# Reordering the hand-over from S to the first block in batch 0 of a fused attention and channel-mix kernel

**Chip and metric.** One core of one Trainium2 chip. PE is the matrix engine (TensorE) and PEld its weight load, DVE VectorE, ACT ScalarE, POOL GpSimd, SP SyncE. All times are device microseconds (us), the time of a run being that of the core from launch to end. The span in a profile, from the first to the last instruction, is about 1.85 us shorter than the time of the same run.

## The reference

Cross-covariance attention on three inputs of 4 x 6208 x 256, followed by a channel mix with a shift by one row:

```
s = (k / |k|)^T (q / |q|)            # 256 x 256 per batch, norms over the rows
a = softmax(s);  x = v @ a           # 6208 x 256 per batch
xk = mu_k*x + (1-mu_k)*x_prev        # x_prev: x, one row later; xr likewise with mu_r
out = sigmoid(xr @ w_r) * (relu(xk @ w_k)**2 @ w_v)     # w_k 256 x 1024, w_v 1024 x 256
```

Nothing of x can be had before S of that batch is complete. For batches 1 to 3 the kernel computes S beside the blocks of the batch before. For batch 0 there is nothing to work on beside it, so the time between the last row of S and the first full stream of matmuls is spent waiting. The change is about that time.

## The kernel before

S of batch 0 is summed in 14 row groups: 0 is the 64 rows left over, 11 (`DIRECT`) the last full one, 12 and 13 (`LAST`) are of half size. What the change touches:

```python
# the last group: q and k diagonals, norms, then the off-diagonal part of S
if last:
    for s in range(n):
        for ih in range(2):          # L192: q and k diagonal
            ...
    diagonal()                       # DVE: sum of q squares from the diagonal
    norms_last()                     # PE: k squares of the last group
for s in range(n):
    for ih in range(2):              # L199: off-diagonal
        ...
def norms_first():                   # called before the cast of the last group
    bank[0] = ps.tile([P, 8], F32, name="bank", tag="xT_ps", bufs=2)
    for h in range(2): nc.tensor.matmul(bank[0][:, h:h + 1], rowsum["acc"][...], ones_f, ...)
    for g in [0] + list(range(DIRECT, LAST)):
        norms_of(g)
... # (cut)
root(1); root(0)                                   # ACT: square roots of the norms
nc.scalar.activation(gate, ones[:, 0:1], AF.Exp)   # ACT: loads exp's table
nc.tensor.transpose(bank[0][:, 4:8], mu_rows, ident_f[:4, :4])
keep_warm(2)                                       # PE: junk matmuls
turn_half, take_half = v_first()
invert_first(0)                                    # DVE
evac_first()                                       # DVE: S, times 1/|q|, out of PSUM
turn_half(0)                                       # PE: first half of v's block 0 turned
turn()                                             # PE: S turned
turn_half(1)
go = v_transpose_pe(1, nc.scalar.copy)             # PE: v's block 1 turned; go() is its copy, on ACT
keep_warm(3)
invert_first(1)
take_half(0, nc.vector.tensor_copy)
nc.vector.tensor_copy(mu_t, bank[0][:, 4:8])
nc.vector.tensor_scalar_add(less, mu_t, -1.0)
difference(0)                                      # DVE: v minus the row before, first half
exp()                                              # ACT
take_half(1, nc.scalar.copy)
go()
weigh_first(0); weigh_first(1)                     # DVE: softmax weights a_sb
difference(1)
for a in range(2):                                 # two halves of the first block's 512 rows
    for ih in range(2): product(a, ih)             # PE: x_ps; ACT: xT from it
    for dh in range(2): mix_first("xk", a, dh)     # DVE: xk
```

After this come the first matmuls with w_k ("up"). The results (`res`) of the first blocks are held back (`HOLD = 4`) and stored from about 95 us on, so that their stores stay out of the way of the loads.

## Time and profile before

| | before |
|---|---|
| time | 505.73 (median of 3 runs, 505.73 to 505.91) |
| profiled run | 505.47, span 503.7 |
| PE busy | 479.2 of 503.7 us (95%) |
| first matmul of group 11 | 32.59 |
| up matmul after the last wait of the hand-over | 49.52 |

Two lines of the profile's page of the kernel before, busy time by engine and the shares of the chain that ended last:

```profile
PE 479.2 (95%) x3372; PEld 331.1 (66%) x3432; DVE 428.9 (85%) x790; ACT 428.7 (85%) x870; POOL 97.0 (19%) x143
PE 90%; DMA 4%; ACT 2%; DVE 2%; issue 1%; SPq 0%; ACTq 0%; DVEq 0%
```

PE is the bound, and what can be gained lies where PE isn't. (3372 matmul records against 3432 weight loads: some matmuls are missing from this trace, so its PE share reads a little low.) Two moments serve as marks below. "Start" is the first matmul of group 11, which comes when the loads and casts let it. "**Hand-over**" is the time from there to the first matmul of block 1's up product after its xk (`49.52 PE kT_ps` in the chain of waits of before): 49.52 - 32.59 = 16.93. From there on PE hardly waits.

### The profile page before, as it was taken

To read this page: it belongs to the slowest core of one execution; us is meant where nothing else is said; L and a number is where in the kernel's file an instruction comes from. 1 tells how busy PE (TensorE), PEld (TensorE's weight loads), DVE (VectorE), ACT (ScalarE), POOL (GpSimd) and SP (SyncE) were. 2 spreads that over 40 slices of the span, in tenths; PEclk is the share of its full clock that TensorE was granted. 3 is DMA by queue.
4 is the path that set the end of the run, shared out by engine and by line. 5 is a ranking of instruction groups with operands and counts; after the bars stand their busy time and mean duration, and the time that the engine had idled before them with its cause. 6 is when DMAs were issued, how large, how long until landed. Compare 5 with 4: busy or idle time off the path is not lost.

```text
span 503.7 us, 9236 instructions
## 1 busy us (share of the span) xinstructions
PE 479.2 (95%) x3372; PEld 331.1 (66%) x3432; DVE 428.9 (85%) x790; ACT 428.7 (85%) x870; POOL 97.0 (19%) x143
## 2 busy tenths in 40 slices
PE   2689999999999999999999999999999999999996
PEld 1345677677666666776676676666666666666675
DVE  2778899999988998899889899899888787878784
ACT  4778999899989989888999898988888878788784
POOL 0044332222233122122123322110031010000000
PEclk9999999999999999999999999999999999999999
DMA  8999999999799999997799999983295857345123
GB/s 332 417 309 189 197 191 176 193 203 213 149 180 176 209 164 175 148 205 117 140 196 140 197 173 185 162 144 75 64 201 102 161 88 152 78 103 88 55 72 105
DMA packets 131558, 83.46 MB, mean 166 GB/s; under 512 B 50548, under 2 KB 125624, under 8 KB 130488
## 3 DMA queue, kind: packets, MB, share of 16 engines
q0 software_dynamic: 55840, 33.01, 49.4%
q1 hardware_dynamic: 75352, 49.59, 40.4%
q8 instruction: 27, 0.44, 0.4%
q10 hardware_dynamic: 320, 0.26, 0.2%
q14 instruction: 19, 0.16, 0.1%
HBM read 78.71 MB, written 25.43 MB: 207 GB/s over the span
## 4 chain that ended last, share of the span: by engine, by line
PE 90%; DMA 4%; ACT 2%; DVE 2%; issue 1%; SPq 0%; ACTq 0%; DVEq 0%
PE vr_ps L598 33%; PE kT_ps L566 30%; PE vr_ps L594 10%; PE xT_ps L460 8%; PE s_ps L288 6%; DMA f<-in_k_dram 4%; ACT k L160 1%; ACT qk L155 1%; PE s_ps L199 1%; PE st_ps L348 0%; PE y_ps L638 0%; DVE xk L551 0%; DVE k L167 0%; DVE kk L579 0%; ACT kr L508 0%
## 5 line engine op out<-in xcount | busy, mean ns | idle before, releaser
L571 ACT ACTIVATE kr<-kT_ps 128x512 bf16<-128x512 f32 (+1 forms) x390 | 234.7, 604 | 33.6 <-PE kT_ps L566 29.8
L598 PE MATMUL vr_ps<-w_v_sb,kk 128*128 128x256 bf16 x1536 | 230.3, 273 | 0.1
L566 PE MATMUL kT_ps<-xk,w_k_sb 128*128 128x512 bf16 (+1 forms) x721 | 217.3, 377 | 0.4 <-DVE xk L551 0.2
L598 PEld LDWEIGHTS <-kk 128*128 128x128 bf16 x1536 | 150.3, 98 | 57.3
L579 DVE TENSOR_TENSOR kk<-kr 128x2048 bf16<-128x2048 bf16 (+1 forms) x148 | 125.7, 850 | 0.2 <-ACT kr L571 0.2
L608 DVE SCALAR_TENSOR_TENSOR res<-res,vr_ps 128x256 f32<-128x256 f32 x192 | 79.9, 416 | 50.6 <-ACT res L607 50.6
L566 PEld LDWEIGHTS <-w_k_sb 128*128 128x128 bf16 x780 | 75.5, 98 | 27.5 <-issue 0.6
L607 ACT ACTIVATE res<-vr_ps 128x256 f32<-128x256 f32 x192 | 76.6, 399 | 1.3 <-PE vr_ps L598 1.3
L594 PE MATMUL vr_ps<-w_r_sb,xr 128*128 128x256 bf16 x384 | 73.3, 273 | 2.8
L462 ACT CAST xT<-xT_ps 128x512 bf16<-128x512 f32 x94 | 55.8, 594 | 20.0 <-PE xT_ps L460 19.7
L551 DVE SCALAR_TENSOR_TENSOR xr<-delta,mu_t,xT 128x512 bf16<-128x512 bf16 x94 | 70.0, 745 | 0.0
L551 DVE SCALAR_TENSOR_TENSOR xk<-delta,mu_t,xT 128x512 bf16<-128x512 bf16 x94 | 69.9, 745 | 0.0
L594 PEld LDWEIGHTS <-xr 128*128 128x128 bf16 x384 | 37.6, 98 | 44.5 <-issue 0.2
L133 POOL DMA_DIRECT2D qk<-in_q_dram x39 | 26.0, 667 | 169.5 <-ACT kr L571 152.1
L460 PE MATMUL xT_ps<-vT,a_sb 128*128 128x512 bf16 x188 | 55.9, 379 | 0.0
L288 PE MATMUL s_ps<-qk 128*128 128x256 bf16 (+1 forms) x294 | 55.8, 273 | 0.0
L249 ACT ACTIVATE sq<-qk 128x1024 bf16<-128x1024 bf16 x48 | 51.0, 1062 | 0.0
L403 POOL DMA_DIRECT2D v_bf<-in_v_dram x47 | 35.7, 761 | 66.4 <-DMA vT<-v_bf 49.5
L199 PE MATMUL s_ps<-qk 128*128 128x384 bf16 (+2 forms) x98 | 19.7, 347 | 16.1 <-ACT qk L155 15.3
L541 DVE TENSOR_TENSOR delta<-xT 128x1024 bf16<-128x1024 bf16 x47 | 32.2, 686 | 1.1 <-ACT xT L462 1.1
L288 PEld LDWEIGHTS <-qk 128*128 128x128 bf16 (+1 forms) x294 | 28.5, 98 | 5.6 <-issue 0.8
L133 POOL DMA_DIRECT2D qk<-in_k_dram x39 | 25.9, 664 | 4.0 <-DMA w_k_sb<-in_moe_w_k_dram 2.7
(114 smaller groups left out, 252.3 us busy)
## 6 DMA issues: line engine op xcount, KB each, us to landing
out_dram<-res SPq DMA_DIRECT2D x47, 512.0 KB, 4.8
v_bf<-in_v_dram POOLq DMA_DIRECT2D x47, 256.0 KB, 7.6
qk<-in_q_dram POOLq DMA_DIRECT2D x36, 256.0 KB, 5.8
qk<-in_k_dram POOLq DMA_DIRECT2D x36, 256.0 KB, 7.4
f<-in_q_dram SPq DMA_DIRECT2D x4, 1024.0 KB, 13.1
f<-in_k_dram SPq DMA_DIRECT2D x4, 1024.0 KB, 11.0
f<-in_q_dram SPq DMA_DIRECT2D x3, 512.0 KB, 7.7
f<-in_k_dram SPq DMA_DIRECT2D x3, 512.0 KB, 6.1
```

The source lines that it names most:

```text
L133: nc.gpsimd.dma_start(rows_at(qk, b, g, i)[:rows, :n], qk_src(t, b, g))
L288: nc.tensor.matmul(s_ps[:, ih, :], rows_at(qk, b, g, 0)[:rows, s, ih * P:(ih + 1) * P], rows_at(qk, b, g, 1)[:rows, s, :], start=t0 and ih ...
L460: nc.tensor.matmul(xT_ps, a_sb[:, b, ih, dh * P:(dh + 1) * P], vT[:, :, ih, :], start=ih == 0, stop=ih == 1)
L462: nc.scalar.copy(xT[:, dh, 1:], xT_ps)
L551: nc.vector.scalar_tensor_tensor(o[:, dh], st[i, "d"][:, dh], mu[:, dh:dh + 1], st[i, "x"][:, dh, :M], op0=OP.mult, op1=OP.add)
L566: nc.tensor.matmul(kT_ps[:, :m], w_k_sb[:, dh, fh * P:(fh + 1) * P], xk[:, dh, :m], start=dh == 0, stop=dh == 1)
L571: nc.scalar.activation(kr, kT_ps[:, :m], AF.Relu, scale=0.5 ** 0.5)
L579: nc.vector.tensor_tensor(st[i, "kk"][:, fh // 4 * 4 + lo:fh + 1, :m], kr, kr, op=OP.mult)
L594: nc.tensor.matmul(vr_ps[:, D:], xr[:, dh, s * P:(s + 1) * P], w_r_sb[:, dh, :], start=dh == 0, stop=dh == 1)
L598: nc.tensor.matmul(vr_ps[:, :D], kk[:, fh, s * P:(s + 1) * P], w_v_sb[:, fh, :], start=fh == 0, stop=fh == 7)
L607: nc.scalar.activation(res[:, s], vr_ps[:, D:], AF.Tanh, scale=0.5)
L608: nc.vector.scalar_tensor_tensor(res[:, s], res[:, s], 1.0, vr_ps[:, :D], op0=OP.add, op1=OP.mult)
```

## The change

Five moves: (1) the norm matmuls of all groups up to 11 before S of group 12 rather than after it; (2) in the last group the norms of groups 12 and 13 and the turn of mu behind the q diagonal, with mu copied by ACT from a bank of its own, and the off-diagonals ordered by half; (3) both halves of v turned ahead of S, the second copied by ACT before exp rather than after; (4) x by output half, and the second xT copied as two halves; (5) three junk matmuls fewer.

```diff
+        for s, ih in [(s, ih) for ih in range(2) for s in range(n)] if last else \
+                [(s, ih) for s in range(n) for ih in range(2)]:      # off-diagonals by half
...
-        for g in [0] + list(range(DIRECT, LAST)):
+        for g in (0, DIRECT):
             norms_of(g)
...
-        norms_of(LAST)
+        mu_ps = ps.tile([P, 4], F32, name="mu_ps", tag="kT_ps", bufs=3)
+        nc.tensor.transpose(mu_ps, mu_rows, ident_f[:4, :4])
+        for g in range(DIRECT + 1, LAST + 1):
+            norms_of(g)
+        nc.scalar.copy(mu_t, mu_ps)
+        nc.vector.tensor_scalar_add(less, mu_t, -1.0)
...
-            for t, src in zip(pairs[a], (...)):
-                for dh in range(2):
+            for dh in range(2):
+                for t, src in zip(pairs[a], (...)):
                     nc.tensor.matmul(t[:, dh], a_sb[...], src, ...)
             if ih:
-                for dh in (0, 1) if a == 0 else (slice(0, 2),):
+                for dh in (0, 1):
                     nc.scalar.copy(xT[...], pairs[a][0][:, dh])
...
-        if g == LAST:
-            norms_first()
         group_cast(g, pending)
+        if g == DIRECT + 1:
+            norms_first()
...
-    nc.tensor.transpose(bank[0][:, 4:8], mu_rows, ident_f[:4, :4])
-    keep_warm(2)
...
     turn_half(0)
+    turn_half(1)
+    take_half(1, nc.scalar.copy)
     turn()
-    turn_half(1)
+    keep_warm(2)
     go = v_transpose_pe(1, nc.scalar.copy)
-    keep_warm(3)
     invert_first(1)
     take_half(0, nc.vector.tensor_copy)
-    nc.vector.tensor_copy(mu_t, bank[0][:, 4:8])
-    nc.vector.tensor_scalar_add(less, mu_t, -1.0)
     difference(0)
     exp()
-    take_half(1, nc.scalar.copy)
     go()
```

More of the change, by code (lines that the diff above doesn't have):

```diff
@@ L195, in cov_first @@
             norms_last()
-        for s in range(n):
-            for ih in range(2):
-                c = slice(P, 3 * P) if last else slice(ih * P, ih * P + 3 * P)
-                nc.tensor.matmul(cov[0][ih][:, c], row[:rows, s, at[ih]:at[ih] + P], row[:rows, s, c],
-                                 start=g == 1 and s == 0, stop=last and s == n - 1, skip_group_check=True)
+        for s, ih in [(s, ih) for ih in range(2) for s in range(n)] if last else \
+                [(s, ih) for s in range(n) for ih in range(2)]:
+            c = slice(P, 3 * P) if last else slice(ih * P, ih * P + 3 * P)
+            nc.tensor.matmul(cov[0][ih][:, c], row[:rows, s, at[ih]:at[ih] + P], row[:rows, s, c],
+                             start=g == 1 and s == 0, stop=last and s == n - 1, skip_group_check=True)
     def norms_first():
-        bank[0] = ps.tile([P, 8], F32, name="bank", tag="xT_ps", bufs=2)
+        bank[0] = ps.tile([P, 4], F32, name="bank", tag="xT_ps", bufs=2)
         for h in range(2):
@@ L479, in product @@
                               for tag, bufs in ((("vr_ps", 2), ("vr_ps", 2)), (("s_ps", 1), ("xT_ps", 2)))[a]])
-            for t, src in zip(pairs[a], (vT0[:, ih, a * H + 1:(a + 1) * H + 1], dv[:, ih, a * H:(a + 1) * H])):
-                for dh in range(2):
+            for dh in range(2):
+                for t, src in zip(pairs[a], (vT0[:, ih, a * H + 1:(a + 1) * H + 1], dv[:, ih, a * H:(a + 1) * H])):
                     nc.tensor.matmul(t[:, dh], a_sb[:, 0, ih, dh * P:(dh + 1) * P], src,
```

## The prediction

> **What bounds the kernel now.** I read the page first, then the chain of waits in order of time from 0 to 75 us, then the timelines of single engines from 32 to 50 us. From about 49.5 us to the end the chain is PE, one matmul after another, with pieces of "issue" of 0.05 us. Before 32 us it is loads and casts. The diff touches only what lies between: the hand-over of batch 0 from S to the first block. What it saves there moves the whole PE-bound rest forward, if nothing between 42 and 49.5 us holds it back.
>
> The end of S, in PE's timeline:
>
> ```profile
> 33.40 1.45 PE L199 MATMUL s_ps<-qk 128*128 128x384 bf16 x7
> 34.69 0.50 PE L206 MATMUL bank<-ones_f,k_acc 128*128 128x1 f32 x4
> 35.13 0.20 PE L217 MATMUL bank<-ones,k_left 64*128 64x1 bf16 x2
> 35.26 0.45 PE L217 MATMUL bank<-ones,k 128*128 128x1 bf16 x12
> 35.57 0.38 PE L192 MATMUL s_ps<-qk 128*128 128x128 bf16 x4
> 35.79 0.24 PE L217 MATMUL bank<-ones,k 128*128 128x1 bf16 x4
> ```
>
> The norm matmuls (L206, L217) stand between the last full groups of S and the q diagonal (L192), although the last cast (DVE L157, 34.26 for 0.41 us) has been done since 34.67. The diagonal feeds the rest.
>
> The same stretch on ACT:
>
> ```profile
> 36.07 0.17 ACT L317 ACTIVATE rn<-bank 128x2 f32<-128x2 f32 x1 [1.14 <-PE bank L217]
> 36.49 0.20 ACT L317 ACTIVATE rn<-rn 128x2 f32<-128x2 f32 x1 [0.24 <-DVE dg L313]
> 36.71 1.28 ACT L734 ACT_TABLE_LOAD   x1
> 38.00 0.21 ACT L734 ACTIVATE gate<-ones 128x1 bf16<-128x1 bf16 x1
> 38.61 0.47 ACT L356 ACTIVATE e_sb<-st_ps,rn 128x256 f32<-128x256 f32 x1 [0.40 <-PE st_ps L348]
> ...
> 39.95 0.59 ACT L442 COPY vT<-vT_ps 128x512 bf16<-128x512 bf16 x1 [0.32 <-DVE sm L368]
> 40.43 1.02 ACT L428 COPY vT<-vT_ps 128x1024 bf16<-128x1024 bf16 x1
> 41.33 1.40 ACT L486 CAST xT<-x_ps 128x256 bf16<-128x256 f32 x3
> ```
>
> ACT is the path from 39.95 to 41.33: it copies the second half of v and block 1's v before the first x. And on DVE:
>
> ```profile
> 38.83 0.42 DVE L442 COPY vT<-vT_ps 128x512 bf16<-128x512 bf16 x1 [0.48 <-PE vT_ps L439]
> 39.17 0.15 DVE L747 COPY mu_t<-bank 128x4 f32<-128x4 f32 x1
> 39.36 0.17 DVE L748 TENSOR_SCALAR less<-mu_t 128x4 f32<-128x4 f32 x1
> 39.44 0.42 DVE L474 TENSOR_TENSOR delta<-vT 128x512 bf16<-128x512 bf16 x1
> 39.77 0.16 DVE L368 RECIPROCAL sm<-sm 128x1 f32<-128x1 f32 x1
> 39.97 0.35 DVE L369 TENSOR_SCALAR a_sb<-e_sb,sm 128x256 bf16<-128x256 f32 x1
> 40.23 0.15 DVE L368 RECIPROCAL sm<-sm 128x1 f32<-128x1 f32 x1
> 40.42 0.35 DVE L369 TENSOR_SCALAR a_sb<-e_sb,sm 128x256 bf16<-128x256 f32 x1
> ```
>
> exp had delivered its first sum by 39.17, but DVE reaches its reciprocal at 39.77: copy, mu, less and delta stand in the queue before it.
>
> **The Trainium skill.** "PSUM — Partial Sum Buffer", section "PSUM bank collisions raise a hardware error", has two engines kept apart by bank and quadrant, "not by address". The trace agrees in effect: the off-diagonal matmul at 36.29 waits for DVE's read of other columns of the bank, and the copy at 38.83 of half 0 waits for PE's turns of half 1. I use this three times. "TensorE: Matmul & The Clock Gate", section "The HAM clock gate", has a whole idle window of some 3.4 us bring the clock down; here it stays at 1.00 in every 2 us from 36 to 52 with PE idle 0.5 us at most, and the change removes three of five junk matmuls, so this bears on a rival. "ScalarE: Activation LUTs", section "What ACT_TABLE_LOAD costs", measures about 1283 ns; the trace has 1.28.
>
> **Part by part.** All in us; the new times are estimates from the durations and start-to-start distances of the trace.
>
> *Norms sooner.* Eight matmuls of group 11 run from 32.59 at 0.162; group 12's four start only at 34.05, on a cast ending 33.99. So PE idles about 0.16, which the early norms fill. They take 34.69 to 35.46, so 0.77, of which the hole swallows 0.16; the four of group 12 (4 x 0.025 = 0.10) go behind the diagonal. New: 33.89 + 0.77 = 34.67, then 4 x 0.162, so the diagonal starts at 35.32 instead of 35.57: **0.26 sooner**, not the 0.88 that the norms occupy, since most only trade places with other PE work.
>
> *Behind the diagonal* come the mu turn (about 0.16 to the next matmul, as at 36.92) and eight norm columns (0.25): the first root starts near 36.1, as before. The second needs the diagonal at 36.49 - 0.26 = 36.23; the mu copy and the root ahead of it cost some 0.03. Both mu rows have landed at 34.3 by the trace's record, so nothing waits. The second root is at **36.26, 0.23 sooner**. Off-diagonals by half save about 0.1 on PE, but they end before the evacuation, which waits for the root: nothing.
>
> *Both halves of v ahead of S.* The second half of v, issued at 32.68, lands near 36.8, so its turns run at 36.87 to 37.1, before S needs PE (37.74 - 0.23). ACT: table, gate (37.77), then take_half(1) at 37.99; its distance to the next was 0.48, so exp starts at 38.47 rather than 38.61. ACT's table load is now the bound there. exp ends near 39.5, and the 1.02 copy of block 1's v starts there, not at 40.43: ACT is free at 40.4, 0.9 sooner.
>
> *DVE then is the path.* take_half(0) reads the same bank and tile as take_half(1), so it starts at 37.99 + 0.59 + 0.03 = 38.61. Before: 38.83. mu and less, worth 0.18 (delta could have begun at 39.26, not 39.44), are gone from here. delta 39.07, sm 39.41 (+0.34), a_sb 39.60 (+0.19), second a_sb 40.06 (+0.46). Against 39.97 and 40.42 that is **0.36 sooner**. The first x of the second input half runs at 40.47 (0.41 after a_sb).
>
> *x by output half.* ACT waits for a whole bank. x's second half used to be the second matmul of that group and becomes the third (+0.11). So xT starts at 40.47 + 0.23 + 0.27 + 0.04 = 41.01 (before 41.33), xk at 41.44 (before 41.76): the order costs 0.11. For a = 1, the last x matmul ends near 41.85 (before 42.10), and xT split in two lets the third xk start after 0.40 instead of 0.59. The third and fourth xk are 0.44 sooner: 42.32 and 42.72 for 42.76 and 43.16. The fourth one releases the matmul at 43.69, after which kr, xT, delta (46.32), kk and xk (48.06) follow without slack to PE at 49.52. So **0.44** reaches the PE-bound part.
>
> Sum: 0.23 (diagonal and root) + 0.13 (DVE queue; the rest of what it gains is given back waiting for ACT's copy) - 0.04 (wait for the third matmul, net of PE being free sooner) + 0.12 (split xT) = 0.44. 505.73 - 0.45 = **505.28 us**, 0.09%.
>
> **Rivals.**
> 1. *w_k takes over.* It is issued at 34.10 and lands late:
>
> ```profile
> w_k_sb<-in_moe_w_k_dram POOLq DMA_DIRECT2D x1, 512.0 KB, 7.8
> ```
>
> That is 41.95, and the first up matmul runs at 42.30. If the two copies don't wait for each other or xT needs one matmul only, xk would come 0.6 to 0.9 sooner and w_k would cap the gain near 0.6: 505.1. Against it: the waits by bank seen above. In my main case w_k lands about as the first xk ends, 41.93, and the second matmul still waits for its xk.
> 2. *The mu turn holds the roots.* Mu and eight norms now stand before the first root, which stands before the second on ACT's queue. If fp32 turn and wait cost 0.3 more than I took, all the diagonal's gain is lost: 505.5. For it: fp32 matmuls here are slow to be followed (0.18 after L206).
> 3. *PE cools down* without three junk matmuls: a microsecond or more at half clock, 506.5 or above. Against it: PE still works in every microsecond; no gap should exceed 1.0.
> 4. *Hidden anyway*: a load due between 44 and 50 us ends the wait instead. Against it: block 2's v lands at 46.4 and is turned at 47.66, w_v at 49.0 and is first used at 50.8; both have over 0.7 of slack.
>
> **Range and chances.** Rivals 1 and 2 set the edges of the range: 504.90 to 505.60; runs of before spread 0.18. Rival 3 or something unseen is most of what lies outside. 2% is 10 us, far beyond anything in 10 us of hand-over: faster 0.005, same 0.985, slower 0.01.
>
> **What would show it.** Right: the diagonal (L192) starts near 35.3; the second root near 36.25; no gap but the table load between the root and exp on ACT; DVE's copy L442 starts just after ACT's copy L442 ends; the first xk at about 41.4, PE's clock 1.00 throughout, and the first matmul after the last wait at about 49.1. Wrong: the first root after 36.3 (rival 2); the first up matmul waiting for w_k's load with xk long done (rival 1); a clock under 1.00 at 36 to 44 us (rival 3); or 0.4 sooner at 43.5 us and nothing at 50 (rival 4).

## The result

| | before | changed |
|---|---|---|
| time, same rounds | 505.82 (4 runs, 505.73 to 505.98) | 505.62 (4 runs, 505.10 to 506.12) |
| ratio | 1 | 0.9996, 95% interval 0.9978 to 1.0013 |
| profiled run: time, span | 505.47, 503.7 | 505.44, 503.7 |

A ratio here and below is the mean time of one kernel's fast runs over that of the other's of the same rounds, so not quite the ratio of the medians quoted. The median lies just above the range of the prediction (504.90 to 505.60), and a gain of 0.2 us isn't clear of the noise. Striking beside it: the changed kernel's four runs spread over 1.0 us, those of before over 0.25.

The page of the changed kernel, the same two lines:

```profile
PE 481.4 (96%) x3429; PEld 330.8 (66%) x3429; DVE 429.0 (85%) x789; ACT 428.8 (85%) x872; POOL 97.3 (19%) x143
PE 87%; DMA 6%; ACT 3%; DVE 2%; issue 1%; SPq 1%; ACTq 0%; DVEq 0%
```

PE is no busier in truth (3429 records are seen here of what was 3372 there). The new thing is in the chain: DMA's share has grown from 4% to 6%. A DMA has entered the chain of waits where the prediction saw matmuls alone. In the chain itself (start, us, what) it is a turn of v (`vT`), issued at 113.25 and landed at 129.97:

```profile
113.25 16.72 DMA vT<-v_bf
```

First the hand-over. PE's timeline of the changed kernel (start, duration, engine, line, operation; all line numbers of this kernel are some 5 higher than in before from L200 on):

```profile
34.92 0.81 PE L199 MATMUL s_ps<-qk 128*128 128x384 bf16 x4
35.57 0.39 PE L192 MATMUL s_ps<-qk 128*128 128x128 bf16 x4
35.89 0.22 PE L223 MATMUL mu_ps<-ident_f,mu_rows 4*128 4x4 f32 x1
36.04 0.35 PE L217 MATMUL bank<-ones,k 128*128 128x1 bf16 x8
```

The diagonal follows S of group 12 (34.92) at once, and mu and the rest of the norms come behind it. It starts at 35.57, to the hundredth where it was before. But this run's loads came later: its group 11 began at 32.84, not 32.59. Measured from there the diagonal is at 2.73 instead of 2.98. This is why all marks below are counted from that start.

ACT of the changed kernel:

```profile
38.00 0.21 ACT L739 ACTIVATE gate<-ones 128x1 bf16<-128x1 bf16 x1
38.11 0.57 ACT L447 COPY vT<-vT_ps 128x512 bf16<-128x512 bf16 x1
38.61 0.47 ACT L361 ACTIVATE e_sb<-st_ps,rn 128x256 f32<-128x256 f32 x1
...
39.58 1.01 ACT L433 COPY vT<-vT_ps 128x1024 bf16<-128x1024 bf16 x1
41.13 0.65 ACT L491 CAST xT<-x_ps 128x256 bf16<-128x256 f32 x2 [0.54 <-PE x_ps L487]
```

The second half of v is copied before exp and not after, and it starts only 0.11 after the gate starts, although the gate takes 0.21: neighbours on ACT overlap. ACT then waits 0.54 for PE before the first xT; it is no longer the path. DVE is:

```profile
38.72 0.43 DVE L447 COPY vT<-vT_ps 128x512 bf16<-128x512 bf16 x1 [0.20 <-ACT vT L447]
...
39.71 0.37 DVE L374 TENSOR_SCALAR a_sb<-e_sb,sm 128x256 bf16<-128x256 f32 x1
40.18 0.35 DVE L374 TENSOR_SCALAR a_sb<-e_sb,sm 128x256 bf16<-128x256 f32 x1
41.54 1.75 DVE L498 SCALAR_TENSOR_TENSOR xk<-x_ps,less,xT 128x256 bf16<-128x256 f32 x4 [0.67 <-ACT xT L491]
```

All marks counted from the first matmul of group 11, with the prediction's times minus 32.59 (its frame) for comparison:

| mark | before | predicted | changed |
|---|---|---|---|
| q diagonal, PE L192 | 2.98 | 2.73 | 2.73 |
| first root, ACT | 3.48 | about 3.5 | 3.58 |
| second root, ACT | 3.89 | 3.67 | 3.65 |
| ACT's copy of v's second half | 7.35 | 5.40 | 5.27 |
| exp, ACT | 6.02 | 5.88 | 5.77 |
| DVE's copy of v's first half | 6.24 | 6.02 | 5.87 |
| second a_sb, DVE | 7.83 | 7.47 | 7.33 |
| first xT, ACT | 8.74 | 8.42 | 8.28 |
| fourth xk, DVE | 10.57 | 10.13 | 9.97 |
| hand-over | 16.93 | 16.49 | 16.33 |

The last mark in the chains of before and of the changed kernel (start, us, what):

```profile
49.52 0.38 PE kT_ps L566
```

```profile
49.17 0.38 PE kT_ps L571
```

The hand-over went as foretold and then some: 0.60 shorter, not 0.44. And yet the last result of the full blocks started on DVE at 497.92 against 497.93 in before (below, "last result"). 0.25 of the 0.60 was gone before it began (the later start). The rest was lost later. ACT's timeline of the changed kernel at 114 us:

```profile
114.28 0.38 ACT L612 ACTIVATE res<-vr_ps 128x256 f32<-128x256 f32 x1 [1.03 <-DMA out_dram<-res]
```

ACT waited 1.03 us for the store of an earlier, held result to leave the buffer that it wanted. In before no engine waits for a store between 100 and 145 us. The store is only part of it: counted from result 20, results 24 to 27 come 1.13 later than in before, but from result 28 on only 0.20 is left of that. The turned v of the chain above adds the rest. I mark this stretch by DVE's result number 20, counted from 0 (near 104 us), and number 36 (near 144): it takes 40.33 in before and 40.68 in the changed kernel. From result 36 to the last it is 353.67 in both. (In all eighteen profiles below it is 353.67 or 353.68, and 54.40 from the end of the hand-over to result 20.)

So the last result of every profile can be put together from three terms and a constant: last result = start + hand-over + late loss + 448.41, where **late loss** is what the stretch takes beyond 40.33, and 448.41 comes from before (497.93 - 32.59 - 16.93). For the changed kernel: 32.84 + 16.33 + 0.35 + 448.41 = 497.93, measured 497.92. The experiments check this sum and ask what each term depends on.

### The profile page after: what moved, and what is told of

The parts are those of the page before. It is cut to its first block, busy times and chain, and to the rows that moved or that the text cites. A ratio compares the mean times of both kernels' runs of the same rounds, so it can differ in the third digit from the quotient of the medians.

```text
span 503.7 us, 9289 instructions
## 1 busy us (share of the span) xinstructions
PE 481.4 (96%) x3429; PEld 330.8 (66%) x3429; DVE 429.0 (85%) x789; ACT 428.8 (85%) x872; POOL 97.3 (19%) x143
## 4 chain that ended last, share of the span: by engine, by line
PE 87%; DMA 6%; ACT 3%; DVE 2%; issue 1%; SPq 1%; ACTq 0%; DVEq 0%
PE vr_ps L603 32%; PE kT_ps L571 32%; PE vr_ps L599 8%; PE xT_ps L465 8%; PE s_ps L293 6%; DMA vT<-v_bf 3%; DMA f<-in_k_dram 3%; ACT k L160 1%; ACT qk L155 1%; SPq L125 1%; PE s_ps L199 0%; PE y_ps L643 0%; DVE xk L556 0%; PE st_ps L353 0%; DVE k L167 0%
## 5 line engine op out<-in xcount | busy, mean ns | idle before, releaser
L571 PE MATMUL kT_ps<-xk,w_k_sb 128*128 128x512 bf16 (+1 forms) x780 | 230.0, 377 | 0.2 <-DVE xk L556 0.2
```

Source lines behind the costliest of these rows:

```text
L571: nc.tensor.matmul(kT_ps[:, :m], w_k_sb[:, dh, fh * P:(fh + 1) * P], xk[:, dh, :m], start=dh == 0, stop=dh == 1)
```

## The experiments

Two theories on the missing gain: **A**, that transfers fall behind by chance in either kernel, and **B**, that the earlier hand-over brings this about. The first account of all profiles (us; "time" is that of the profiled run itself):

| kernel | start | hand-over | late loss | sum + 448.41 | last result | time |
|---|---|---|---|---|---|---|
| before | 32.59 | 16.93 | 0 | 497.93 | 497.93 | 505.47 |
| null | 32.63 | 16.92 | 0 | 497.96 | 497.95 | 505.59 |
| null2 | 32.81 | 16.96 | 0 | 498.18 | 498.18 | 505.72 |
| null3 | 32.98 | 17.00 | 0 | 498.39 | 498.38 | 506.03 |
| null4 | 32.93 | 17.17 | 0 | 498.51 | 498.50 | 506.06 |
| null5 | 32.84 | 16.93 | 0 | 498.18 | 498.17 | 505.75 |
| null6 | 32.94 | 16.93 | 0 | 498.28 | 498.27 | 505.84 |
| cut_before | 33.04 | 16.92 | 0 | 498.37 | 498.36 | 505.97 |
| changed, first | 32.84 | 16.33 | 0.35 | 497.93 | 497.92 | 505.44 |
| again | 32.73 | 16.81 | 1.72 | 499.67 | 499.65 | 507.25 |
| again2 | 32.97 | 16.37 | 0 | 497.75 | 497.74 | 505.28 |
| cut_after | 32.72 | 16.54 | 0.49 | 498.16 | 498.15 | 505.67 |
| more | 32.81 | 16.32 | 0 | 497.54 | 497.53 | 505.04 |
| joint | 32.83 | 16.85 | 0 | 498.09 | 498.09 | 505.64 |
| x_order | 32.74 | 17.18 | 0 | 498.33 | 498.32 | 505.86 |
| norms_only | 32.49 | 16.68 | 0.72 | 498.30 | 498.28 | 505.82 |
| turn_only | 32.73 | 16.81 | 0.80 | 498.75 | 498.75 | 506.36 |
| best | 32.75 | 16.21 | 0 | 497.37 | 497.36 | 504.90 |

The sum holds within 0.02 for all eighteen, so up to the last result the three terms are all there is. From there to the time of the run it is another 7.51 to 7.65.

### null and again: both kernels unchanged, once more

No edit; both kernels again, in the same rounds, to see how far each repeats.

> The kernel before again, for the spread. Theory A (what the changed kernel lost between 104 and 141 us is chance: a backlog of transfers that comes and goes from run to run): the time spreads by up to 1 us here too, 505.2 to 506.3, and some profile of it shows waits for a store or for a turned v between 90 and 145 us. Theory B (the change itself brings the backlog on): spread stays near 0.25 us around 505.8, and its profile has no such wait. From the first matmul of group 11 to the last wait before the PE-bound part (the up matmul at 49.52) it takes 16.93 us again.

> The changed kernel again. Both theories: from the first matmul of group 11 to the up matmul after the last wait 16.33 us, 0.60 less than before (49.17 - 32.84 against 49.52 - 32.59). Theory A: the backlog is not the same as in its first profile, and the median is some 0.3 to 0.6 us under that of the kernel before once the runs are more than four. Theory B: the same waits between 104 and 141 us again, and a median within 0.2 us of before.

Measured: null 506.07 (five runs, 505.59 to 506.93), ratio 1.0011 (0.9998 to 1.0024); again 505.52 (six runs, 504.95 to 507.25), ratio 1.0003 (0.9989 to 1.0017); before beside them 505.69 (11 runs). So the kernel before doesn't repeat within 0.18 us, as its first three runs made me think. By the letter, null's spread fits theory A; again's median, 0.17 under before, and its wait for a store fit theory B. The changed kernel reaches 504.95, which before never does, and 507.25, which before doesn't either. The profile fell on that 507.25. PE's timeline of again at the first up matmuls, and ACT's at 116 us:

```profile
42.73 0.61 PE L511 MATMUL kT_ps<-xk,w_k_sb 128*128 128x256 bf16 x4 [0.78 <-DMA w_k_sb<-in_moe_w_k_dram]
```

```profile
116.15 0.39 ACT L612 ACTIVATE res<-vr_ps 128x256 f32<-128x256 f32 x1 [2.54 <-DMA out_dram<-res]
```

Two waits, each for a DMA. The first is rival 1 of the prediction: w_k landed at 42.68, the first xk was there, and the hand-over took 16.81 instead of 16.33. The second cost 1.72: results 24 to 27 come 2.64 later, and 0.93 of that is caught up by result 28.

The kernel before has the first wait too, with next to no harm. PE's timeline of null:

```profile
42.64 0.61 PE L506 MATMUL kT_ps<-xk,w_k_sb 128*128 128x256 bf16 x4 [0.29 <-DMA w_k_sb<-in_moe_w_k_dram]
```

Here w_k landed at 42.59, and the hand-over is 16.92 all the same, because the fourth xk comes at 10.57 and the path runs through it. In eight profiles of before, w_k lands 9.1 to 10.1 after the start; the latest (null2) costs its hand-over 0.03. In the changed kernel a landing at 9.41 (more) costs nothing, one at 9.44 (again2) 0.04, with block 1's v holding the fourth xk back by the same 0.04, and one at 9.95 (again) 0.48. The change took the slack that hid it.

### norms_only and turn_only: one part of the change alone

```diff
 # norms_only: before, and only
-        for g in [0] + list(range(DIRECT, LAST)):
+        for g in (0, DIRECT):
-        norms_of(LAST)
+        for g in range(DIRECT + 1, LAST + 1):
+            norms_of(g)
-        if g == LAST: norms_first()
         group_cast(g, pending)
+        if g == DIRECT + 1: norms_first()
 # turn_only: before, and only
-    keep_warm(2)
     turn_half(0)
-    turn()
     turn_half(1)
+    take_half(1, nc.scalar.copy)
+    turn()
+    keep_warm(2)
     go = v_transpose_pe(1, nc.scalar.copy)
-    keep_warm(3)
...
-    take_half(1, nc.scalar.copy)
```

> Only the early norms, mu and v as before. My prediction's step: the diagonal's first matmul 0.26 sooner after group 11's first matmul (2.72 us instead of 2.98), the second root 0.26 sooner, and, since ACT then waits for exp's operand anyway and every later step hangs on it, 0.2 to 0.26 sooner at the up matmul after the last wait (16.67 to 16.73 us). Rival (ACT and DVE queues after exp hide it, as they are in the same order): under 0.1.

> Only the order of v's turns and copies and the junk matmuls; norms, mu and x as before. My theory: the diagonal is not moved (2.98), ACT's copy of v's second half now ends before exp, so exp starts some 0.1 us later after the second root than before (2.12 us from root to exp before), the first a_sb waits for it, and the up matmul after the last wait comes 0.1 to 0.3 us sooner since ACT's long copy is gone from the path. Rival (the long ACT copy was the whole path): 0.45 or more.

Measured: norms_only 505.62 (ratio 1.0001), turn_only 505.65 (1.0002), both within noise of before. By the hand-over each gains: norms_only 16.68, so 0.25 sooner, just what the diagonal gained; turn_only 16.81, so 0.12. Together 0.37 of 0.60. The remaining 0.23 is left to mu off DVE's queue, the split xT and x by output half; x_order and joint below show the last two alone (-0.11 and 0.20), no run shows mu alone. One expectation of turn_only failed: from the second root to exp it takes 2.12 as before, not 0.1 more. And each lost its gain again on the way, in the same place. ACT's timelines of norms_only and of turn_only:

```profile
114.79 0.38 ACT L608 ACTIVATE res<-vr_ps 128x256 f32<-128x256 f32 x1 [1.54 <-DMA out_dram<-res]
```

```profile
115.25 0.38 ACT L607 ACTIVATE res<-vr_ps 128x256 f32<-128x256 f32 x1 [1.63 <-DMA out_dram<-res]
```

Late losses of 0.72 and 0.80.

### cut_before and cut_after: the first eight stores cut to one row

Their outputs are wrong, which doesn't matter for the times. What waits for a held result's store should then wait no more.

```diff
-                    nc.sync.dma_start(*stores.pop(0))
+                    to, frm = stores.pop(0)
+                    few[0] += 1
+                    nc.sync.dma_start(*((to[0:1, 0:1], frm[0:1, 0:1]) if few[0] <= 8 else (to, frm)))
```

> The kernel before with its first eight stores (issued from 94 us on) cut to one row, so their 4 MB do not move; the result is wrong on purpose. Theory A (chance decides in each run whether the transfers fall behind from about 55 us on; where they do, block 6 waits for a held result's store and the gain of the hand-over is used up): everything to 94 us as before, 16.93 us to the up matmul after the last wait; no wait for a store whether or not the transfers are behind; 505.4 to 505.6 with little spread, since the profiles of before had no such wait anyway. Theory B (the stores are not the cause, other transfers are): spread of over 1 us remains.

> The changed kernel with the same cut; the result is wrong on purpose. Theory A: the hand-over's gain, 0.5 to 0.6 us where w_k lands in time and about 0.1 where it lands late, stays to the end: median 504.9 to 505.4, some 0.3 to 0.5 under the cut kernel before, and no run over 505.8. Theory B: runs over 506 remain and the two cut kernels have the same median within 0.1.

Measured: cut_before 506.07 (ratio 1.0009, 0.9993 to 1.0024), no sooner than before, which missed what I expected of it; cut_after 505.58 (0.9997, 0.9983 to 1.0010), above the 504.9 to 505.4 that theory A had expected. The 0.49 between them is near the gain in hand-over, but no more than a hint, as the intervals overlap. The profiles say more. cut_before had no late loss; its profiled run (505.97) is long by its start, at 33.04 the latest of all. In cut_after the waits for stores are gone and the late loss is still 0.49: in its table of waits PE now waits 0.3 us for turned v (`vT`), another transfer. Its chain goes through that turn of v (92.67 to 109.88). So stores are not the only thing that comes late; turned v does too.

cut_after's hand-over of 16.54 has a cause of its own: its chain of waits (start, us, what) comes from block 1's v. Beside it the same place in null4, of which more below:

```profile
33.53 6.09 DMA v_bf<-in_v_dram
```

```profile
33.73 6.10 DMA v_bf<-in_v_dram
```

Both landed 6.90 after the start, 39.62 and 39.83, and both cost about the same: 0.21 to cut_after's hand-over (16.54 for 16.33) and 0.24 to null4's (17.17 for 16.93). This sensitivity, unlike that to w_k, is old.

### x_order: x in the order of before

```diff
-            for dh in range(2):
-                for t, src in zip(pairs[a], (...)):
+            for t, src in zip(pairs[a], (...)):
+                for dh in range(2):
```

> The changed kernel with only the order of the x matmuls of before (both halves of x, then both of its difference). My prediction had the new order cost 0.11 because a copy waits for the whole bank: so the first xT copy and the first xk come 0.11 sooner after group 11's first matmul than the changed kernel's 8.28 and 8.69, that is at 8.17 and 8.58. Rival (the copy waits for its own half): they come no sooner or later by up to 0.11. At the fourth xk (9.97) little is left of either, as DVE has become the bound there: 9.86 to 9.97.

From the second a_sb to the first xT takes 0.84, against 0.95 in the changed kernel: the order "by output half" costs 0.11, as the prediction had it. The 0.11 is still there at the fourth xk (2.53 against 2.64 from the second a_sb), where the expectation had thought it hidden. The gain isn't seen in the time, since two loads came late. ACT's and PE's timelines of x_order:

```profile
38.53 0.59 ACT L447 COPY vT<-vT_ps 128x512 bf16<-128x512 bf16 x1 [0.43 <-PE vT_ps L444]
```

```profile
43.11 0.61 PE L511 MATMUL kT_ps<-xk,w_k_sb 128*128 128x256 bf16 x4 [0.60 <-DMA w_k_sb<-in_moe_w_k_dram]
```

The second half of v landed at 38.05, where it lands between 36.8 and 37.7 in all other profiles. Its turn now stands ahead of S on PE, so exp was 0.51 later than in the changed kernel (6.28 for 5.77). w_k at 43.06 came on top. The hand-over of 17.18 is the longest of all, by 0.01 over null4, and its chain leads to w_k, which set it. What turning both halves ahead of S risks is the other part: the fourth xk at 10.40 instead of 9.97.

### best: a version meant to beat both

The changed kernel with x in the order of before, w_k in two tiles and two loads of half the size (the first up matmuls need the first half only), and two more tiles for held results.

```diff
-    w_k_sb = const.tile([P, 2, DF], BF16, name="w_k_sb")
+    w_k_sb = [const.tile([P, 2, DF // 2], BF16, name=f"w_k{n}_sb") for n in range(2)]
...
-    nc.gpsimd.dma_start(w_k_sb, moe_w_k.rearrange("(ko ki) f -> ki ko f", ki=P))
+    for n in range(2):
+        nc.gpsimd.dma_start(w_k_sb[n], moe_w_k.rearrange(...)[:, :, n * DF // 2:(n + 1) * DF // 2])
...
+            extra = name == "res" and extras[0] > 0     # the first two res tiles
+            t = pn.tile(shape, dtype, name="res_x", tag="res_x", bufs=2) if extra else \
...
-    HOLD = 4                                            # and max(0, i - 3)
+    HOLD = 6                                            # and max(0, i - 5)
```

> A version meant to beat both: the changed kernel with the x order of before, w_k loaded in two tiles (the half that the first up matmuls need first), and two more result tiles with two more blocks held, so that a store has some 30 us to land instead of 10. Theory A: w_k's first half lands near 40 us and is never waited for, the up matmul after the last wait comes at 16.2 to 16.35 us in every run, no block waits for a store: median 504.8 to 505.1, spread under 0.5. Theory B: the hand-over is as said, but the median stays at 505.4 or more with runs over 506.

Measured: 504.90 (five runs, 504.59 to 505.63) against 505.68, ratio 0.9986 (0.9974 to 0.9999), correct. It is the only kernel here whose interval lies below 1, by a hair. The first half of w_k landed at 41.01 (before: 41.95 for the whole), no up matmul waits for it, the hand-over is 16.21 and the late loss 0. The expected spread of under 0.5 was missed (1.04). From the second a_sb to the first xT it takes 0.84 and to the fourth xk 2.53, as in x_order, so the 0.11 or 0.12 by which its hand-over beats 16.32 and 16.33 is accounted for by the order of x: that part of the change was a loss. What its other parts are worth, one profile can't tell.

### null2 and again2: both unchanged, with five rounds

> The kernel before a further time, to see whether its transfers too fall behind. Theory A (chance for both kernels; the hand-over of before has slack for its loads, that of the changed kernel has none): 16.93 us from group 11's first matmul to the up matmul after the last wait whatever the landing of v and w_k, up to about 42.6 for w_k; the stretch from result 20 to result 36 takes 40.33 us where the transfers keep up and 0.3 to 1.7 more where they do not. Theory B (only the changed kernel's transfers fall behind): 40.33 again.

> The changed kernel a further time. Theory A: from group 11's first matmul to the up matmul between 16.33 us (all loads in time) and 17.2, and in each case longer by what it waits for the second half of v, block 1's v or w_k; the stretch from result 20 to result 36 between 40.33 and 42.1. Median over all runs 0.1 to 0.4 under before. Theory B: the stretch is longer than 40.33 again.

Measured: null2 505.74, ratio 0.9999; again2 505.38 (504.88 to 505.75), ratio 0.9989 (0.9977 to 1.0001); before 505.86. This time no run of the changed kernel ran late, and its profile has a late loss of 0 with the hand-over of 16.37. So the late loss isn't part of the change itself; it comes and goes.

### more: one more tile for results; joint: the second xT in one copy

```diff
 # more: the changed kernel, and
+            extra = name == "res" and "res" not in halves
+            t = pn.tile(shape, dtype, name="res_x", tag="res_x", bufs=1) if extra else \
 # joint: the changed kernel, and
-                for dh in (0, 1):
+                for dh in (0, 1) if a == 0 else (slice(0, 2),):
```

> The changed kernel with one more result tile, held as before, so a store has some 30 us to land where it had 10; w_k and x as in the changed kernel. Theory A: no block waits for a store; the stretch from result 20 to 36 is 40.33, or at most 0.5 more from a turned v that comes late; runs over 506 are gone; median 504.9 to 505.4. Rival (late turned v and POOL's loads are what costs, not the stores): the stretch keeps over 0.7 of loss in a profile where transfers are behind, and runs over 506 remain.

> The changed kernel with the copy of x's second half undivided, as before. My prediction had the split worth 0.12 at the fourth xk: from the second a_sb to the fourth xk 2.64 us in the changed kernel, so 2.76 here. Rival (DVE is the bound there and the split is hidden): 2.64 to 2.66.

Measured: more 505.14 (six runs; five from 504.99 to 505.36 and one of 507.29), ratio 0.9992 (0.9978 to 1.0007); joint 505.69, 0.9997. The extra tile didn't keep the one run of 507.29 away; that run wasn't profiled. Its clock is on record as 0.995, where every other clock on record here is 0.998 or more; whether the clock or a wait made it late isn't shown. In the profile that there is, transfers were on time, so it doesn't say what the tile is worth. For joint the fourth xk is at 10.17 instead of 9.97: the split copy is worth 0.20 there. How much of it reached the hand-over stays open, since w_k landed late in that run (42.83) and set it at 16.85.

### null3 to null6: does the kernel before fall behind too?

Four more profiles of the kernel before, one time each, for the question of A or B.

> Four looks at the kernel before, unchanged, for its profile: how often do its transfers fall behind from 55 us on? The mark is the time from the issue to the landing of block 4's v: 10.73 to 10.76 us where they do not (three profiles of before with full stores, joint, more, x_order), 11.2 to 12.2 where they do (all other kernels, cut_before among them, which is the kernel before up to its first store near 95 us). Theory A, chance for either kernel: at least one of the four shows 11.2 or more, and a profiled time of 506 or more goes with a wait of ACT for a store of a held result between 104 and 141 us. Theory B, only the earlier hand-over brings it: all four at 10.73 to 10.76 and no such wait, whatever the time.

> As for the first of the four. Hand-over at 16.9 in any case; time 505.4 to 505.8 if the stretch from result 20 to result 36 takes 40.33 us.

> As for the first of the four. If the mark is 11.2 or more, theory A expects a stretch from result 20 to result 36 of 40.33 to 42.05 us, as in the changed kernel's five profiles; theory B expects 40.33.

> As for the first of the four. Under theory A with the changed kernel's own share of marked profiles (four of five) all four unmarked has a chance of 0.2 to the fourth power, under 1 per cent; with before's own share so far (one of four) it is 0.75 to the fourth power, about a third.

Measured: 506.03, 506.06, 505.75 and 505.84, with 506.07 for the one run of before beside them. Block 4's v took 10.81, 11.01, 10.77 and 10.73 us to land. None reaches the 11.2 that I had set, so by the letter theory A's mark was missed. But the mark was poorly drawn: null4 did fall behind. The same stretches of the profile, for before, null4, again and more in this order (stretch, length, busy time of PE, PEld, DVE, ACT, POOL, granted clock, DMA share, GB/s; the share sums the times of packets over 16 engines, so it can exceed 1):

```profile
100.00:145.00 45.00, 44.65 (x324) 31.42 (x329) 41.43 (x76) 41.05 (x85) 12.99 (x17) 1.00 1.08 182
```

```profile
100.00:145.00 45.00, 44.97 (x331) 31.47 (x329) 41.41 (x76) 41.06 (x84) 13.00 (x17) 1.00 1.32 211
```

```profile
100.00:145.00 45.00, 43.60 (x317) 30.23 (x316) 40.65 (x74) 39.30 (x80) 12.99 (x17) 1.00 1.34 203
```

```profile
100.00:145.00 45.00, 44.97 (x331) 31.61 (x330) 41.45 (x76) 41.37 (x86) 13.00 (x17) 1.00 1.12 180
```

In before and more the DMA share is 1.08 and 1.12 with some 180 GB/s. In null4 and again it is 1.32 and 1.34 with over 200 GB/s (again2: 1.34, 208). In the 40 us before, from 60 to 100 us, it is the other way round: 152 and 151 GB/s in null4 and again at a share of 1.32 and 1.37, against 186 and 190 at 1.13 and 1.14 in before and more. So packets took longer there and less was moved; the excess after 100 us I read as that backlog being worked off. Turned v then lands in 13.0 us in the median in null4 (90 to 150 us), against 4.8 in before and 14.6 in the changed kernel. So the kernel **before falls behind as well**. But no engine waited for it: null4's late loss is 0, as is again2's.

Theory A's other half fell: the times of 506.03 and 506.06 do not go with a wait for a store. The account explains them, but for 0.10 and 0.01 that lie after the last result, by a late start (32.98 and 32.93 for 32.59) and a longer hand-over (17.00 and 17.17, the chain of waits leading to block 1's v in both). In before, then, times of 506 and above (14 of its 50 runs) can come from the start and the hand-over alone; that the other twelve do is an inference.

**What follows for A and B.** Falling behind does not need the change: cut_before (v of block 4 in 11.92 us, and that kernel is the kernel before up to its first store) and null4 show it. It may still be likelier with the change: under 160 GB/s from 60 to 100 us there are six of the ten profiles with a changed hand-over and one of the eight others (null4). Waiting because of it was seen in 0 of 8 profiles with the hand-over of before (in one of them, cut_before, the stores were cut), and in 5 of 10 in which it was changed in whole or part. If the chance were the same in both, all five would fall among those ten with a chance of C(10,5)/C(18,5) = 252/8568, 3%; but this was counted after the fact, and the ten aren't one kernel. I lean to this: an earlier hand-over makes it likelier that a backlog is felt. It is not shown, and why the transfers fall behind at all is open.

## Why the prediction was wrong

**The bound, and the place of the gain: right.** PE bounds the kernel, and only the hand-over was touched. The clock stayed at 0.998 to 1.000 in every profile, and at 1.00 in every 2 us from 36 to 52 in the changed kernel's, so rival 3 (a cold PE) fell. Rival 4 fell for the hand-over: nothing between 44 and 50 us held it up.

**The steps of the hand-over: right, with two terms mis-sized.**
- The diagonal came 0.25 sooner for 0.26, the second root 0.24 for 0.23. Rival 2 fell: the first root came 0.10 later than before, and there was room for that.
- DVE became the path, and its copy waits for ACT's on the same bank, as reasoned. But the second a_sb came 0.50 sooner where 0.36 was expected (0.23 + 0.13). The term at fault is ACT's: the distance from the gate to the next copy was taken as the gate's duration, 0.22, and it is 0.11. Everything behind it moves by the same amount. The rest are hundredths.
- The -0.04 for the third matmul's wait is what was measured: 0.50 at the second a_sb became 0.46 at the first xT (8.74 - 8.28). x_order confirmed the 0.11 of the order itself.
- The split xT was put at +0.12; from the first xT to the fourth xk the gain grew from 0.46 to 0.60, by 0.14, and joint puts the split alone at 0.20.
- Sum: 0.24 + 0.26 - 0.04 + 0.14 = 0.60, for 0.23 + 0.13 - 0.04 + 0.12 = 0.44. (The prediction then took 0.45 off 505.73; 0.44 gives 505.29.)

**The step that failed: "So 0.44 reaches the PE-bound part", and with it that the hand-over "moves the whole PE-bound rest forward".** In the profiled run the gain at the end of the hand-over was 0.60, and at the last result 0.01: the start was 0.25 later, and 0.35 was lost to waits in the stretch from 104 to 144 us. The gain gets through only in runs in which loads and transfers are on time, which are not all of them. The other three of the four runs in the result have no profile, so the account holds for the one at 505.44, not for the median run by run.
1. Rival 1 was right as a mechanism and too small in extent. It was told as a cap on a larger gain. It is a cap that moves from run to run: w_k lands 9.1 to 10.3 us after the start, and from about 9.4 on it sets the hand-over. Block 1's v did the same in cut_after, and v's second half held back the fourth xk in x_order. Five profiles whose code is the same up to there (changed, again, again2, cut_after, more) have hand-overs of 16.32 to 16.81, so 0.60 to 0.12 is gained.
2. The rest is not PE alone. In half of the profiles with a changed hand-over, waits for stores of held results or for turned v took back 0.35 to 1.72 between 104 and 141 us. The prediction had looked for slack up to 50 us and taken the chain's "PE" after it for an assurance. A chain of PE in one run doesn't show how near the next limit is.
3. The start of the changed kernel's profile was 0.25 later than that of before, on the same loads, which appears in no estimate and is nearly half the gain. This is chance and no effect of the change as far as the profiles show: starts run from 32.59 to 33.04 in the eight profiles with the hand-over of before and from 32.49 to 32.97 in the other ten, and the profile of before was the earliest of its eight.

**The range: wrong in kind.** It was built on rivals inside the hand-over and on the 0.18 by which three runs of before differed. Fifty runs of before spread from 505.39 to 506.93 with a median of 505.74. Fifteen of the changed kernel spread from 504.88 to 507.25 with a median of 505.39; six of them are below 505.3, where none of before is, and three above 506. The difference of the medians, 0.35 sooner, is near what was predicted, but drawing runs anew at random puts it between 0.63 sooner and 0.06 later (95%), so it's likely and not proven; the pool also mixes chips. The median of four runs drawn at random from these fifteen lies between 504.96 and 506.48 (95%), twice as wide as the range given.

## What to carry to other kernels

Take a run's time apart into where it starts, the stretch that you changed and what is lost afterwards, and compare these, not the totals: gains of tenths are plain there when the time shows nothing. When you shorten a stretch, list the loads and stores that come due in and after it, with their landing times in several profiles: slack that one profile shows is the slack of one run. And take the spread from many runs before setting a range of a few tenths.

## What the Trainium skill lacked or had wrong

- "ScalarE: Activation LUTs", section "What ACT_TABLE_LOAD costs": had it right, and the prediction didn't use this sentence. It says that back-to-back ACTIVATEs overlap by about 93 ns. Here the gate (0.21 us) was followed by a copy 0.11 us after its start, so an overlap of 0.10. The table load of 1.28 agrees as well.
- "PSUM — Partial Sum Buffer", section "PSUM bank collisions raise a hardware error": right, but without a price. Waiting by bank cost 0.11 us here (x by output half, 0.95 for 0.84 from the second a_sb to the first xT), because a reader of one half waits for the matmul of the other.
- "DMA: Bandwidth & Descriptors", section "Why a DMA increments its semaphore by 16 and not by 1": says that engines finish independently and only the full count means landed. Missing is how far apart: in the changed kernel the last of the 16 completions of block 4's v came at 55.67, 1.48 us after the fifteenth; in before it was 0.02.
- No page says how much a landing varies from run to run under load: w_k, issued at 34.0 to 34.6 as one load, landed anywhere from 41.95 to 43.06 in these profiles.
- No page tells of transfers that settle into a backlog for tens of microseconds: turned v landed in 4.8 us in the median in one profile of the kernel before and in 13.0 in another (null4), with the same transfers queued. What sets it off is open here too.
- "TensorE: Matmul & The Clock Gate", section "The HAM clock gate": nothing to add; with three junk matmuls fewer the granted clock was 0.998 or above in every profile.
